# Two decode layers on one core: wq laid out by groups of heads, V 4 and V 5 in unbroken rows, the first K ahead of wq, and K 8 of layer 2 in two transfers

## The chip, the cores and the metric

The kernel runs on one core of a Trainium2 chip. Its time is the device time of one execution in microseconds (us); the time before is the median of three runs. The core has a matrix engine (TensorE, called PE in the profile, with its weight loads as PEld), a vector engine (DVE), a scalar engine (ACT), GpSimd (POOL) and a queue that issues transfers (SP, SPq in the profile). Sixteen DMA engines move data between the device's main memory and the core's on-chip memory, which is addressed by 128 partitions. All transfers of this kernel are issued by SP, in the order in which its instructions stand.

## The reference: what is computed

One token (a row of 640 numbers) goes through two equal layers. Every layer is an attention over a window of a key/value cache and a small feed-forward mixer. Both layers use the same caches and the same weights, and everything is bf16.

```python
W = 4096                                     # the last 4,096 of 32,768 positions
def _A_ref(x, k_cache, v_cache, wq, wo):     # x [1,1,640], caches [1,32,32768,192]
    q = (x @ wq) -> 32 heads of 192          # wq [640, 6144]
    scores = q . k_cache[head, last W] * 192**-0.5
    p = softmax(scores)
    o = p . v_cache[head, last W]
    return o.reshape(1, 1, 6144) @ wo        # wo [6144, 640]
def _B_ref(x, w1, w2, w3, w4):               # w3 [640, 1536], w4 [1536, 640]
    ...
    return x1 + gelu(layernorm(x1) @ w3) @ w4

x = x + _A_ref(_layernorm(x), ...)           # layer 1
x = x + _B_ref(_layernorm(x), ...)
x = x + _A_ref(_layernorm(x), ...)           # layer 2, the same caches and weights
x = x + _B_ref(_layernorm(x), ...)
```

One head's window of keys is 4,096 x 192 bf16, 1.5 MB, and so is its window of values. Thirty-two heads have 96 MB, two layers 192 MB.

## The kernel before

The code counts layers from 0; this text says layer 1 and layer 2 (`layer == 0` and `layer == 1`). "K 8" is the window of keys of head 8, "V 4" the window of values of head 4.

**Tiles.** A window is kept as a tile of 128 partitions x 6,144 numbers (12,288 B in a partition; partition p has 32 positions that follow each other). Twelve such tiles, the cells, are handed round: a loader takes a free cell (`take`), and the work that reads it last gives it back (`give`). wq has a tile of its own, `wq_sb` (L143): 128 partitions x 5 blocks of rows (kc, 0 to 4) x 6,144 columns, 61,440 B in a partition. The 6,144 columns are 8 groups (c, 0 to 7) of 768, four heads each. In the order before, a partition holds kc first and the columns second, so that one group's columns are five pieces of 1,536 B, 12,288 B apart.

**The work of a group.** The query of four heads is projected from wq's columns of that group (`qproj_steps`), the keys of each head are transposed in place on DVE (L534), multiplied with the query on PE (L620), the softmax of the four heads is taken, and the values are summed with its weights (`pv`, L761). wo's rows of the group finish it. Layer 1 takes the groups from 7 down to 0, layer 2 from 0 up to 7.

**What layer 2 finds in place.** Layer 1 ends with heads 0 to 7, and layer 2 begins with them. Their eight K stay in cells as they are. Of the V, V 2 and V 3 stay whole, V 1 and V 4 in part: of V 4 only the first 1,536 of its 6,144 columns have to be loaded again. The space for that, and for V 5, is wq's own: once layer 2 has projected group 0 and then group 1, their columns of wq are not used any more. `fill_hole` (L188) puts three transfers there, at places that `hole` (L182) finds: V 4's 1,536 columns into the first two pieces of group 0's space, V 5's first 2,304 columns into the other three, V 5's other 3,840 columns into the five pieces of group 1's space. Called V 4, V 5a and V 5b below.

**How transfers are issued.** Three forms stand in the code. The plain one, `nc.sync.dma_start`, reads and writes one run for each partition. `load_wide` (L48) joins four partitions' rows into one run of the source, 49,152 B, and spreads it over four partitions. `load_runs` (L59) reads one run for each partition and writes it as several pieces of 1,536 B. Whole cells and wq's blocks kc 1 to 4 go by `load_wide`, wq's block kc 0 and K 8 of layer 2 (`load_k`, L171, with `NKEEP` = 8) by the plain form, and the three parts of V 4 and V 5 by `load_runs`.

**The order.** `stream` (L385) is a written-out list of loads; `need` walks it and issues each item when the program comes to it. It begins with wq's block 0, x, wq's blocks 1 to 4, then K 28, K 29 and so on. An issue waits until its cell is free (for PE and DVE, by semaphores) and until the transfer eight places before it has landed, as eight semaphores are used in turn. At the change of layers the order is: w3 and w4 of layer 1's mixer, V 0 in two halves, two parts of V 1 (3,072 and 768 B in a partition), V 4, V 5a, K 8, K 9, K 10, V 5b, V 6. V 4 and V 5a wait for the projection of layer 2's group 0 (L565), K 8, K 9 and K 10 for the scores (L620) of heads 0, 1 and 2, whose cells they take, and V 5b for the projection of group 1.

Of the kernel before, what the change touches and what calls it, by code (L numbers as in the profile page):

```python
# [9 lines left out]
BF16 = mybir.dt.bfloat16  # L10
# [8 lines left out]
P = 128  # L19
# [29 lines left out]
def load_wide(nc, dst, src):  # L49


    wide = src.rearrange("(g w) n -> g (w n)", w=WIDE)
    assert [list(d) for d in wide.ap] == [[WIDE * src.shape[1], P // WIDE], [1, WIDE * src.shape[1]]]
    sym = [mybir.BassSymbolicTensorAccessPattern(ap=a.ap, dtype=a.dtype, bass_ap=a) for a in (wide, dst)]
    return nc.sync.add_instruction(mybir.InstDMACopy(
        name=nc.get_next_instruction_name(), ins=sym[:1], outs=sym[1:], queue="qSPDynamicHW", mode="Copy"))


def load_runs(nc, dst, src):  # L59

    sym = [mybir.BassSymbolicTensorAccessPattern(ap=a.ap, dtype=a.dtype, bass_ap=a) for a in (src.unsqueeze(1), dst)]
    return nc.sync.add_instruction(mybir.InstDMACopy(
        name=nc.get_next_instruction_name(), ins=sym[:1], outs=sym[1:], queue="qSPDynamicHW", mode="Copy"))
# [3 lines left out]
def kernel(  # L67
# [14 lines left out]
    nc = tc.nc  # L82
    shrink_ring(nc)
    _, _, D = A_x.shape
    _, H, Sk, Dh = A_k_cache.shape
    W = min(4096, max(256, Sk // 4))
    F = B_w3.shape[1]
    HD = H * Dh
# [3 lines left out]
    ND, NF = D // P, F // P  # L92
# [3 lines left out]
    NG = H // QH  # L96
    QC = QH * Dh
    QT = QC // P
# [3 lines left out]
    FREE = NT * HALF  # L102
    scale = float(Dh) ** -0.5
    eps = 1e-5
    s0 = Sk - W
# [3 lines left out]
    NKEEP, NCELL = 8, 12  # L109
# [9 lines left out]
    GROUPS = [[list(range(h, h + QH)) for h in range(0, H, QH)] for _ in range(2)]  # L119
# [9 lines left out]
    fixed = ctx.enter_context(tc.tile_pool(name="fixed", bufs=1))  # L129
# [10 lines left out]
    nc.scalar.add_instruction(mybir.InstLoadActFuncSet(  # L140
        name=nc.get_next_instruction_name(), act_func_set_id=ACT_TABLE_SET, ins=[], outs=[]))

    wq_sb = fixed.tile([P, ND, HD], BF16, name="wq_sb")  # L143
    wx_sb = fixed.tile([P, (ND - W3C) * F + (NF - W4C) * D], BF16, name="wx_sb")

    kx = fixed.tile([P, NKX * Dh], BF16, name="kx")
# [7 lines left out]
    def take(key):  # L154
        i = free.popleft()
        cell_of[key] = i
        return (low if i == NCELL - 1 else cells).tile([P, FREE], BF16, tag=f"cell{i}", name=f"cell{i}")
# [4 lines left out]
    def load(dst, src, wide=True):  # L162
        (partial(load_wide, nc) if wide else nc.sync.dma_start)(dst, src)
# [6 lines left out]

    def load_k(layer, h):  # L171
        t = take(("k", layer, h))
        load(t[:], A_k_cache[0, h, s0:Sk, :].rearrange("(p j) d -> p (j d)", p=P), (layer, h) != (1, NKEEP))
        return t

    SLOT = 2 * Dh
    HOLE = ND * QC
# [1 line left out]
    VYA = HOLE - (FREE - VN)  # L179
    assert QC == 2 * SLOT and (FREE - VN) % QC == 0 and VYA < FREE <= VYA + HOLE  # L180

    def hole(i):  # L182

        c, i = divmod(i, HOLE)
        k, i = divmod(i, QC)
        return wq_sb[:, k, c * QC + i:c * QC + i + SLOT]

    def fill_hole(i, src):  # L188
        c, i = divmod(i, HOLE)
        k, n = i // QC, src.shape[1] // QC  # L190
        assert i % QC == 0 and n * QC == src.shape[1] and k + n <= ND
        load_runs(nc, wq_sb[:, k:k + n, c * QC:(c + 1) * QC], src)

    def load_hole(layer, h):

        src = A_v_cache[0, h % H, s0:Sk, :].rearrange("(p j) d -> p (j d)", p=P)
        if h == VX:
            fill_hole(0, src[:, 0:FREE - VN])
            return hole
        if h == VY + H:  # L200
            fill_hole(FREE - VN, src[:, 0:VYA])
        else:
            fill_hole(HOLE, src[:, VYA:])
        return lambda i: hole(i + FREE - VN)
# [46 lines left out]
        return V[:, i:i + n]  # L251

    def load_wq(layer, kc):
        load(wq_sb[:, kc, :], A_wq[kc * P:(kc + 1) * P, :], kc > 0)
        return wq_sb

    def load_wo(layer, c):
# [32 lines left out]
    def load_w4(layer):  # L290
# [38 lines left out]
        return block  # L329

    LOADERS = {"x": load_x, "k": load_k, "v": load_v, "wq": load_wq, "wo": load_wo, "fill": fill_wo, "w3": load_w3, "w4": load_w4}

    def layer_stream(layer):
# [48 lines left out]
            assert seq[0:4] == [("v", 1, 0), ("v", 1, 1), ("v", 1, VX), ("v", 1, VY + H)]  # L382
        return seq

    stream = [("wq", 0, 0), ("x",)] + [("wq", 0, kc) for kc in range(1, ND)] + layer_stream(0) + layer_stream(1)  # L385
    pos = [0]

    def need(*key):
        while key not in loaded:
            k = stream[pos[0]]  # L390
            pos[0] += 1
            loaded[k] = LOADERS[k[0]](*k[1:])
        return loaded[key]
# [146 lines left out]
    def qproj_steps(c, xc, part=None, row=None):  # L540


        held = {}
        n = QT if part is None else QT // 2
        t0 = c * QT + (part or 0) * n

        def project():
            need("wq", 0, ND - 1)
            if row is not None:
                N = QC // 2  # L550
                qr_ps = psm.tile([33, N], F32, tag="psm")
                for kc in range(ND):
                    for i in range(2):
                        nc.tensor.matmul(  # L554
                            qr_ps[32 * i:32 * i + 1, :], lhsT=xc[:, kc:kc + 1],
                            rhs=wq_sb[:, kc, t0 * P + i * N:t0 * P + (i + 1) * N],
                            start=(kc == 0), stop=(kc == ND - 1))
                for i in range(2):
                    nc.scalar.copy(row[32 * i:32 * i + 1, :], qr_ps[32 * i:32 * i + 1, :])  # L559
                return  # L560
            qT_ps = psm.tile([P, n], F32, tag="psm")
            for tl in range(n):
                t = t0 + tl
                for kc in range(ND):
                    nc.tensor.matmul(  # L565
                        qT_ps[:, tl:tl + 1], lhsT=wq_sb[:, kc, t * P:(t + 1) * P], rhs=xc[:, kc:kc + 1],
                        start=(kc == 0), stop=(kc == ND - 1))
            held["q"] = qT_ps

        def spread():  # L570
            if row is not None:
                qT_ps = psm.tile([P, n], F32, tag="psm")
                for tl in range(n):
                    i, j = divmod(tl, n // 2)
                    nc.tensor.matmul(qT_ps[:, tl:tl + 1], lhsT=row[:, j * P:(j + 1) * P],  # L575
                                     rhs=Eq[0:33, i, 0:1], start=True, stop=True)
                held["q"] = qT_ps
            Xq = o_bytes[:, 2 * (256 + 2 * QH):][:, 0:4 * n].rearrange("p (t b) -> p t b", b=4)
            nc.vector.tensor_tensor(  # L579
                out=Xq[:], in0=held["q"][:, :].unsqueeze(2).broadcast_to([P, n, 4]),  # L580
                in1=maskq[:, :].unsqueeze(1).broadcast_to([P, n, 4]), op=ALU.mult)
            held["x"] = Xq

        def repeat():
            Qrep_ps = psm.tile([P, 4 * n], F32, tag="psm")
            nc.tensor.matmul(Qrep_ps[:], lhsT=Lb[:], rhs=held["x"][:].rearrange("p t b -> p (t b)"),
                             start=True, stop=True)
            held["r"] = Qrep_ps

        def block():  # L590
            nh = n * P // Dh
            h0 = 4 * (t0 - c * QT) // NCOL
            src = held["r"][:, :].rearrange("p (h f) -> p f h", h=nh)
            pairs = [Qblk[:, c % 2, i:i + QPAIR].rearrange("p (f u b) -> p f u b", u=5, b=NM) for i in (0, QPAIR)]
            outer, inner = slice(0, 5, 4), slice(1, 5, 3)
            if nh == QH:
                parts = (pairs[0][:, :, outer], src[:, :, 0:4:3]), (pairs[1][:, :, inner], src[:, :, 1:3])
            else:
                units = (0, 0), (1, 1), (1, 4), (0, 4)
                parts = [(pairs[k][:, :, u:u + 1], src[:, :, i:i + 1]) for i, (k, u) in enumerate(units[h0:h0 + nh])]  # L600
            for to, q in parts:
                shape = [P, NCOL, q.shape[2], NM]
                nc.vector.tensor_tensor(
                    out=to, in0=q.unsqueeze(3).broadcast_to(shape),
                    in1=blkm[:, :].unsqueeze(1).unsqueeze(1).broadcast_to(shape), op=ALU.mult)

        return project, spread, repeat, block

    def scores(h, K, ST, hq):
# [679 lines left out]
```

## Time and profile before

| | us |
|---|---|
| time, median of 3 runs | 510.49 (510.01 to 510.89) |
| the profiled execution: device time | 509.65 |
| its span, from the first to the last instruction | 507.9 |
| DVE busy in the span | 304.1 (60%) |
| PE busy in the span | 277.7 (55%) |

The page of the profile gives the busy time of each engine, then the span in 40 slices of 12.7 us with the share of time in which the 16 DMA engines were busy and the rate at which they moved data, the DMA queues, the chain of work that ended last, and groups of instructions. Other views answer questions of the trace: the windows view gives busy time, DMA share and rate in stretches that one names, the timeline one engine's instructions in order of time, the DMA view the issues with their size and the median time from issue to landing. In the windows view a packet's bytes are put to the moment at which it begins, so that stretches of 1 us with large packets swing, and stretches of several us are read. The trace also holds a record of each DMA packet, with its beginning, its duration and its size.

### The profile page before, as it was taken

The numbers are of one execution on the slowest core, as the hardware profiler recorded it, in microseconds if no ns is written. First come the engines' busy times: TensorE is split into PE (matmuls) and PEld (weight loads), VectorE is DVE, ScalarE is ACT, GpSimd is POOL, SyncE is SP. The second block draws the span as 40 slices with busy tenths as digits, with TensorE's granted clock in tenths as the row PEclk, the third lists the DMA queues.
The fourth block names the chain that finished last, engine by engine and source line by source line (L and its number), as shares of the span: only waits on it lengthen the run. The fifth ranks groups of instructions, "written<-read, shape, count | busy, mean of one in ns | idle before, by whom it ended". The sixth has DMA issues, their size and how long they took to land. (4 is left out here: it accounts for less than half of the span.)

```text
span 507.9 us, 7504 instructions
## 1 busy us (share of the span) xinstructions
PE 277.7 (55%) x3141; PEld 132.9 (26%) x3141; DVE 304.1 (60%) x508; ACT 54.5 (11%) x179; POOL 3.7 (1%) x16
## 2 busy tenths in 40 slices
PE   1134747536274473853756666647463753637675
PEld 0011313213031131311423543223121221212145
DVE  2076686567674675746735365867766665756532
ACT  1000101011010110100011101011110101001111
POOL 2000000000000000000000000000000000000000
PEclk9995695758767687585775595978877785766655
DMA  9999999999999999999999999999999999999996
GB/s 372 434 434 434 431 442 431 400 430 433 443 432 441 428 421 437 426 411 446 431 389 421 359 396 446 431 430 431 430 425 437 434 423 434 421 448 431 418 401 250
DMA packets 12725, 213.41 MB, mean 420 GB/s; under 512 B 2804, under 2 KB 3444, under 8 KB 8436
## 3 DMA queue, kind: packets, MB, share of 16 engines
q1 hardware_dynamic: 12692, 212.94, 98.6%
q8 instruction: 25, 0.41, 0.3%
q14 instruction: 8, 0.07, 0.0%
HBM read 212.93 MB, written 0.00 MB: 419 GB/s over the span
## 5 line engine op out<-in xcount | busy, mean ns | idle before, releaser
L534 DVE STREAM_TRANSPOSE cell<-cell 128x1536 uint32<-128x1536 uint32 (+1 forms) x83 | 193.3, 2331 | 33.6 <-DMA cell<-in_A_k_cache_dram 32.9
L620 PE MATMUL ST_ps<-cell,Qblk 128*16 128x512 bf16 (+1 forms) x864 | 134.1, 473 | 83.9 <-DVE cell L534 68.3
L761 PE MATMUL O_ps<-cell,PT 128*2 128x384 bf16 x916 | 90.0, 424 | 5.9 <-DMA cell<-in_A_v_cache_dram 2.8
L620 PEld LDWEIGHTS <-Qblk 128*16 128x16 bf16 x864 | 43.9, 104 | 145.3 <-issue 121.3
L770 DVE STREAM_TRANSPOSE o_sb<-O_ps 128x384 f32<-128x384 f32 x60 | 33.8, 563 | 45.5 <-PE O_ps L761 45.5
L783 ACT ACTIVATE words<-oT_ps,words 32x6 bf16<-32x6 f32 x63 | 16.2, 257 | 245.6 <-PE oT_ps L782 149.8
L761 PEld LDWEIGHTS <-PT 128*2 128x2 bf16 x1024 | 34.2, 92 | 30.2 <-issue 19.5
L579 DVE TENSOR_TENSOR o_sb<-qT_ps,words 128x24 bf16<-128x24 f32 (+1 forms) x17 | 3.0, 179 | 47.0 <-PE qT_ps L575 45.7
L657 PE MATMUL pmT_ps<-ident,words 64*1 64x64 f32 (+1 forms) x16 | 4.1, 257 | 42.9 <-DVE words L652 42.8
L554 PE MATMUL qr_ps<-wq_sb,words 128*1 128x384 bf16 x120 | 20.4, 484 | 11.5 <-DMA wq_sb<-in_A_wq_dram 10.5
L782 PE MATMUL oT_ps<-o_sb,Lq 128*32 128x6 f32 x126 | 14.3, 186 | 22.4 <-DVE o_sb L781 22.4
L782 PEld LDWEIGHTS oT_ps<-o_sb,Lq 128*32 128x32 f32 x126 | 12.1, 126 | 40.7 <-issue 26.9
L684 DVE STREAM_TRANSPOSE o_sb<-o_sb 64x512 bf16<-64x512 bf16 (+1 forms) x14 | 9.4, 669 | 19.9 <-ACT o_sb L678 18.6
L809 PE MATMUL yr_ps<-cell,words 128*1 128x320 bf16 x120 | 16.1, 431 | 0.0
L673 PE MATMUL nb_ps<-words,o_sb 1*64 1x1 f32 (+1 forms) x14 | 2.6, 185 | 24.5 <-DVE o_sb L665 24.4
L657 PEld LDWEIGHTS pmT_ps<-ident,words 64*1 64x1 f32 (+1 forms) x16 | 1.2, 77 | 45.4 <-issue 44.3
L652 DVE TENSOR_REDUCE words<-ST_ps 64x1 f32<-64x512 f32 (+1 forms) x16 | 10.3, 643 | 3.6 <-PE ST_ps L620 3.5
L559 ACT CAST wx_sb<-qr_ps 1x384 bf16<-1x384 f32 x16 | 7.5, 468 | 43.9 <-PE qr_ps L554 28.3
L781 DVE TENSOR_TENSOR o_sb<-o_sb 128x6 f32<-128x6 f32 x63 | 10.7, 170 | 2.0
L554 PEld LDWEIGHTS <-words 128*1 128x1 bf16 x120 | 6.6, 109 | 19.6 <-issue 17.1
L678 ACT ACTIVATE o_sb<-ST_ps,o_sb,words 64x512 bf16<-64x512 f32 (+1 forms) x14 | 10.4, 743 | 0.5
L675 ACT COPY o_sb<-nb_ps 64x1 f32<-64x1 f32 (+1 forms) x14 | 2.1, 153 | 74.1 <-PE nb_ps L673 74.1
(184 smaller groups left out, 192.0 us busy)
## 6 DMA issues: line engine op xcount, KB each, us to landing
cell<-in_A_k_cache_dram SPq DMA_DIRECT2D x56, 1536.0 KB, 27.7
cell<-in_A_v_cache_dram SPq DMA_DIRECT2D x53, 1536.0 KB, 27.8
cell<-in_A_wo_dram SPq DMA_DIRECT2D x13, 960.0 KB, 27.7
wq_sb<-in_A_wq_dram SPq DMA_DIRECT2D x5, 1536.0 KB, 12.1
cell<-in_A_v_cache_dram SPq DMA_DIRECT2D x8, 768.0 KB, 15.8
cell<-in_B_w_dram SPq DMA_DIRECT2D x4, 768.0 KB, 9.1
cell<-in_A_wo_dram SPq DMA_DIRECT2D x3, 480.0 KB, 16.9
cell<-in_B_w_dram SPq DMA_DIRECT2D x2, 640.0 KB, 10.1
```

The lines of the kernel that those rows point to most:

```text
L534: nc.vector.transpose(Ku, Ku)
L554: nc.tensor.matmul(qr_ps[32 * i:32 * i + 1, :], lhsT=xc[:, kc:kc + 1], rhs=wq_sb[:, kc, t0 * P + i * N:t0 * P + (i + 1) * N], start=(kc == ...
L620: nc.tensor.matmul(ST_ps[r:r + QW, :].rearrange("p (g j i) -> p g j i", g=ng, j=NJ4), lhsT=Q[n], rhs=T[:, ng * i:ng * (i + 1), :, f, :, t] ...
L652: nc.vector.tensor_reduce(out=pm[S, :], in_=ST_ps, op=ALU.max, axis=AX.X)
L678: nc.scalar.activation(out=Pr, in_=ST_ps, func=ACTF.Exp, bias=nb_sb[:, 0:1], scale=sc[S, 0:1], accum_out=lpart[:, 0:1])
L684: nc.vector.transpose(held["PrT"], held["Pr"])
L761: nc.tensor.matmul(O_ps[r:r + 2, :], lhsT=PT[:, hq, 2 * i:2 * i + 2], rhs=v_pair(V, h, 2 * i * Dh, 2 * Dh), start=(i < 4), stop=(i >= NB - 4))
L770: nc.vector.transpose(o_sb[:], O_ps.rearrange("p (e a c) -> p e c a", e=2, c=NA))
L781: nc.vector.tensor_add(o2, o2, o_sb[:, 1, :, 1])
L782: nc.tensor.matmul(oT_ps[r, :], lhsT=Lq[:], rhs=o2, start=True, stop=True)
L783: nc.scalar.activation(oT[r, :], oT_ps[r, :], ACTF.Copy, scale=rl[r, 0:1])
L809: nc.tensor.matmul(yr_ps[32 * i:32 * i + 1, :], lhsT=oT[:, k:k + 1], rhs=wo_t[:, k * D + i * N:k * D + (i + 1) * N], start=(k == 0), stop= ...
```

## The change

- `wq_sb` becomes 128 partitions x 8 groups x 5 blocks x 768 columns: a partition now holds one group after the other, 7,680 B each. PE reads the same 1,536 B pieces at other places, and the space of a projected group is one unbroken run.
- V 4, V 5a and V 5b then are one run in each partition, of 3,072, 4,608 and 7,680 B, and go by the plain form.
- wq's blocks kc 1 to 4 still go by `load_wide`, and each 49,152 B run of the source is now written as 32 pieces of 1,536 B where it was 4 of 12,288 B. Block kc 0 becomes two transfers: the columns of group 7, 1,536 B in a partition, by the plain form, and the other seven groups by `load_runs`, 10,752 B read and seven pieces written.
- The first K of the stream, K 28, goes ahead of everything, by the plain form where it was wide. x stays second, and then come wq's blocks.
- K 8 of layer 2 becomes two plain transfers, of 3,072 and 9,216 B in a partition.

The instructions of PE, DVE, ACT and POOL and their order are the same. SP issues two transfers more than before.

```diff
@@ load_wide
     wide = src.rearrange("(g w) n -> g (w n)", w=WIDE)
+    wide = wide.unsqueeze(1) if len(dst.shape) == 3 else wide
@@
-    wq_sb = fixed.tile([P, ND, HD], BF16, name="wq_sb")
+    wq_sb = fixed.tile([P, NG, ND, QC], BF16, name="wq_sb")
@@ load_k
         t = take(("k", layer, h))
-        load(t[:], A_k_cache[0, h, s0:Sk, :].rearrange("(p j) d -> p (j d)", p=P), (layer, h) != (1, NKEEP))
+        src = A_k_cache[0, h, s0:Sk, :].rearrange("(p j) d -> p (j d)", p=P)
+        if (layer, h) == (1, NKEEP):
+            for i, e in ((0, FREE // 4), (FREE // 4, FREE)):
+                nc.sync.dma_start(t[:, i:e], src[:, i:e])
+        else:
+            load(t[:], src, (layer, h) != (0, GROUPS[0][0][0]))
         return t
@@
-    def hole(i):
+    def hole(i, n=SLOT):
         c, i = divmod(i, HOLE)
-        k, i = divmod(i, QC)
-        return wq_sb[:, k, c * QC + i:c * QC + i + SLOT]
+        return wq_sb[:, c].rearrange("p k n -> p (k n)")[:, i:i + n]
     def fill_hole(i, src):
-        c, i = divmod(i, HOLE)
-        k, n = i // QC, src.shape[1] // QC
-        assert i % QC == 0 and n * QC == src.shape[1] and k + n <= ND
-        load_runs(nc, wq_sb[:, k:k + n, c * QC:(c + 1) * QC], src)
+        nc.sync.dma_start(hole(i, src.shape[1]), src)
@@
     def load_wq(layer, kc):
-        load(wq_sb[:, kc, :], A_wq[kc * P:(kc + 1) * P, :], kc > 0)
+        rows = A_wq[kc * P:(kc + 1) * P, :]
+        if kc > 0:
+            load_wide(nc, wq_sb[:, :, kc, :], rows)
+        else:
+            nc.sync.dma_start(wq_sb[:, NG - 1, kc, :], rows[:, HD - QC:])
+            load_runs(nc, wq_sb[:, 0:NG - 1, kc, :], rows[:, 0:HD - QC])
         return wq_sb
@@
-    stream = [("wq", 0, 0), ("x",)] + [("wq", 0, kc) for kc in range(1, ND)] + layer_stream(0) + layer_stream(1)
+    seq = layer_stream(0) + layer_stream(1)
+    stream = [seq.pop(0), ("x",)] + [("wq", 0, kc) for kc in range(ND)] + seq
@@ qproj_steps
-                            rhs=wq_sb[:, kc, t0 * P + i * N:t0 * P + (i + 1) * N],
+                            rhs=wq_sb[:, c, kc, i * N:(i + 1) * N],
...
-                t = t0 + tl
+                t = t0 - c * QT + tl
                 for kc in range(ND):
                     nc.tensor.matmul(
-                        qT_ps[:, tl:tl + 1], lhsT=wq_sb[:, kc, t * P:(t + 1) * P], rhs=xc[:, kc:kc + 1],
+                        qT_ps[:, tl:tl + 1], lhsT=wq_sb[:, c, kc, t * P:(t + 1) * P], rhs=xc[:, kc:kc + 1],
                         start=(kc == 0), stop=(kc == ND - 1))
```

## The prediction

> **What bounds the kernel now.** I read the page first: how busy each engine is, the slices, the DMA queues.
>
> ```profile
> span 507.9 us, 7504 instructions
> PE 277.7 (55%) x3141; PEld 132.9 (26%) x3141; DVE 304.1 (60%) x508; ACT 54.5 (11%) x179; POOL 3.7 (1%) x16
> ...
> DMA  9999999999999999999999999999999999999996
> GB/s 372 434 434 434 431 442 431 400 430 433 443 432 441 428 421 437 426 411 446 431 389 421 359 396 446 431 430 431 430 425 437 434 423 434 421 448 431 418 401 250
> ...
> q1 hardware_dynamic: 12692, 212.94, 98.6%
> ```
>
> No engine is over 60% busy, and the DMA engines are busy in every slice: the end is set by 213 MB, their rate and the stretches in which it sinks. The lowest slices are the last (the tail of the last mixer) and the 23rd, 279 to 292 us, the change of layers. The windows view, cut finer there and with two long stretches beside it, gives (after the busy times: PE clock, DMA share, GB/s):
>
> ```profile
> 20.00:260.00 240.00, 128.50 (x1196) 56.82 (x1195) 155.60 (x201) 25.15 (x77) 0.00 (x0) 0.73 1.00 431
> 354.00:480.00 126.00, 68.81 (x661) 28.43 (x655) 82.84 (x110) 12.56 (x40) 0.00 (x0) 0.73 1.00 431
> ```
> ```profile
> 288.00:290.00 2.00, 1.84 (x33) 1.05 (x37) 0.49 (x5) 0.00 (x0) 0.00 (x0) 0.50 0.83 249
> 290.00:292.00 2.00, 2.00 (x42) 1.32 (x34) 0.05 (x1) 0.29 (x2) 0.00 (x0) 0.61 1.02 357
> 292.00:294.00 2.00, 2.00 (x70) 1.45 (x62) 0.69 (x4) 0.18 (x1) 0.00 (x0) 1.00 0.93 239
> 294.00:296.00 2.00, 1.26 (x30) 0.78 (x26) 0.65 (x3) 0.00 (x0) 0.00 (x0) 1.00 0.93 387
> ```
>
> Against 431, 288 to 290 is short of 364 KB (0.84 us), and 290 to 296 of 618 KB (1.43 us). SP's timeline shows what it issued then (start, duration):
>
> ```profile
> 281.40 4.57 SPq L216 DMA_DIRECT2D cell<-in_A_v_cache_dram  x4
> 287.80 1.24 SPq L62 DMA_DIRECT2D wq_sb<-in_A_v_cache_dram  x2
> 289.66 0.34 SPq L163 DMA_DIRECT2D cell<-in_A_k_cache_dram  x1
> 291.18 1.80 SPq L55 DMA_DIRECT2D cell<-in_A_k_cache_dram  x2
> 293.32 0.56 SPq L62 DMA_DIRECT2D wq_sb<-in_A_v_cache_dram  x1
> ```
>
> V 4 goes at 287.80, as soon as PE has projected group 0 (30 matmuls of L565 from 286.91 to 287.85), and takes 0.59 us to issue; V 5a follows at 288.48, 0.55; K 8 at 289.66, when PE is through with head 0. By the packet records most DMA engines have no packet between 288.6 and 289.2. K 8's first packets of 12,288 B begin between 292.2 and 292.8 and take 1.04 to 1.81 us where 0.46 is usual: its data flow from about 292.9, 3.2 us after the issue. At the kernel's start the plain wq block, of the same shape, is issued at 0.74 and flows from about 2.5, 1.8 us later; V 0's second half, issued at 283.84, after 1.9. So K 8 is some 1.3 us late, behind V 4 and V 5a with their 640 pieces. From 300 to 474, by issues against packet records, 16 us and more of transfers are always issued ahead: time that DMA loses here is lost at the end, and time that it wins is kept.
>
> **The change part by part.** Terms are per DMA engine, as all sixteen work side by side.
>
> *V 4 and V 5 plain.* Plain issues (V 0's, L216) take 0.33 us, V 4's 0.59. V 4 stands at the head of an empty queue, so its data come 0.26 earlier: -0.26. Then the 1.43 us. V 5a's packets average 210 ns, 178 without a stall (8 packets, 0.25 us), K 8's 555 against 460 (8, 0.76), and between V 5a's last and K 8's first packet engines stand empty for 0.34 on average: 1.35; the rest is the fixed part of small packets and stays. No row shows K 8 behind two plain transfers here. Bounds: all 1.35 goes, or none. The nearest row is V 1's first part, plain, issued at 285.04 behind plain halves with 2.4 us of transfers ahead (K 8 has 2.3): four engines of sixteen stalled for 0.3 to 0.45 us, 0.13 on average. I take that: -1.22. PE's order and waits are the same, so K 8 can't be issued before 289.66; what is late next is PE's chain from the mixer's last product to the projection, which leaves the remaining 0.6 us of 288 to 290 as it is.
>
> *K 8 in two.* Eight packets more. The line through packets of 1,280 B (55 ns) and 2,560 B (102 ns) leaves 8 ns a packet: +0.06. The second issue costs SP 0.4 us; K 9 stands behind it, at 291.18, and waits for PE. The transposition needs both parts.
>
> *wq in pieces.* V 5b, five pieces a packet, averages 293.6 ns where a plain packet of 7,680 B takes 291: 0.65 ns a further piece. A wide wq packet gets 28 more: 4 transfers x 2 packets x 28 x 0.65 = 0.15; block 0 has 8 packets with 6 more, 0.03, and 8 packets more, 0.06. V 5b itself: -0.02. Bounds for a piece: nothing, or 8 ns, as for a packet of its own (272 pieces, 2.2 us). I take 0.65, from the row of the same form.
>
> The Trainium skill, DMA: Bandwidth & Descriptors, section on the semaphore's increment of 16, says that one descriptor moves one contiguous run, and its table of measured loads has about 10.5 ns a packet; an estimate from these, 3,712 runs more over 16 engines, is 2.4 us, against 0.22 by V 5b's row.
>
> *K 28 first, and plain.* 8 packets of 460 ns for 2 of 1,820: +0.04. x stays second behind 1.5 MB, so DVE's L476 stays at 6.80. wq's last block lands at about 25.3 instead of 21.6 and Qblk is written at 28.1 instead of 24.4. The transposition of K 28 (3.38 us) starts then instead of at 25.30, K 29's ends at 34.9 instead of 32.3; the third started at 34.81 in any case, behind 2.45 us of waiting for ACT. The lag is gone there, and cost nothing while 21 us and more of transfers are issued ahead. SP issues two transfers more before K 29, which waits for K 28 to land (about 7) as it did for wq's block before. The cells go round as before, one transfer ahead in the ring of eight.
>
> Sum: -0.26 - 1.22 + 0.06 + 0.22 + 0.04 = -1.16, some 508.5 on the profiled execution's own 509.65 (span 507.9 and 1.75 around it). That execution lies 0.84 under the median; on the median 510.49 it is 509.3. I call 0.2% (1.0 us) what a measurement here tells from no change.
>
> **The rivals.**
>
> *Pieces are described slower than they are moved* (slower). If K 8 was late because 640 pieces had to be described ahead of it, wq's pieces must be too, 1,024 in a transfer. The 1.3 us over the 384 pieces beyond one a row make 3.4 ns each: 3.5 us a transfer, against 3.64 to move it, and K 28 gives a lead of some 2.7. That just holds; it turns at 3.5 ns. Counted from V 4's issue to 1.0 us before K 8's first packet (the delay at the kernel's start), 288.0 to 291.2, all time to 640 pieces, it is 5 ns: 5.1 us a transfer, 1.5 late four times, 1.3 in block 0, less the lead: 4.6 later, less the gain of 1.2 at the change of layers: 513.9. Halfway between the two prices, 511.6. For it: the two prices stand so near to each other. Against: issue takes 0.55 to 0.59 us for two, three and five pieces a row alike.
>
> *K 8's stall is its own* (no change): engines that run dry need a microsecond to restart, whatever was ahead. Then -0.26 and +0.32 remain: 510.55. Against: V 1 and V 0 restarted in half the time.
>
> The Trainium skill, Perfetto Trace Analysis, HWDGE's DMA instruction, says that descriptors are generated within the issue's profiled span; by that V 5a was described by 289.03, and this rival would hold. The start of the kernel, 0.6 us from the issue's end to the first packet, can't decide it.
>
> *Each piece costs like a packet* (slower): 2.2 us for 0.18, 511.3. Against: V 5b's row. For it: that row was behind others, at a rate of 424 GB/s, and has five pieces where wq has 32. The Trainium skill's figure above belongs here.
>
> **How the numbers follow.** The forecast, 509.3, has 0.54, of which 0.42 lies over 0.2% faster; descriptions too slow 0.24; K 8's own stall 0.13; dear pieces 0.07; 0.02 for other gains. So faster 0.44, same 0.24, slower 0.32. The forecast's own range is 508.6 to 510.1 (all of the stall gone and free pieces, to half of it). The range reaches past the middle of the slower rival: 508.6 to 512.6 leaves out some 0.06 below and 0.14 above.
>
> **What would show it.** Right: windows 290 to 296 at 400 GB/s or more, K 8's first data within 2 us of its issue, plain issues of 0.33 us at V 4 and V 5a, 3 to 25 us at 430 as before, wq's last block landing at about 25.3. Wrong: slices 1 and 2 below 430 with wq's transfers 4 to 5 us apart (pieces described too slowly), wide wq packets well over 1.84 us (dear pieces), or K 8's first packets again over 1 us with the same hole at 292 (its own stall).

## The result, and the profile after

The changed kernel takes 511.33 us (median of 21 runs, 510.47 to 512.05), the kernel before 510.22 in the same comparison (21 runs, 509.38 to 512.13). The ratio is 1.0016, with a 95% interval from 1.0009 to 1.0023: 0.5 to 1.2 us slower. The forecast was 509.3, 1.2 us faster. A later comparison of the same two kernels gave 1.0014 (1.0002 to 1.0027).

The page of the changed kernel: busy engines, slices, DMA queue.

```profile
span 508.9 us, 7508 instructions
PE 282.7 (56%) x3141; PEld 135.9 (27%) x3141; DVE 303.5 (60%) x508; ACT 54.6 (11%) x179; POOL 3.7 (1%) x16
...
DMA  9999999999999999999999999999999999999995
GB/s 371 425 433 433 434 390 435 442 433 430 444 427 433 431 427 410 433 430 449 430 387 420 357 406 441 447 431 415 433 434 444 422 430 433 412 435 430 424 409 226
...
q1 hardware_dynamic: 13076, 212.94, 98.6%
```

The DMA engines are still the bound, and the 23rd slice, the change of layers, is still low: 357 GB/s for 359. The second slice, 13 to 25 us, has fallen from 434 to 425. The windows view of the changed kernel, in the stretches that the prediction read (the sixth row is the three before it together), and from 6 to 25 us, where wq moves behind K 28 (the kernel before has 456 there, but its large packets begin elsewhere at the edges; the lag below is the cleaner measure):

```profile
20.00:260.00 240.00, 129.43 (x1190) 57.90 (x1189) 154.96 (x200) 25.19 (x77) 0.00 (x0) 0.72 1.00 429
288.00:290.00 2.00, 1.73 (x49) 1.27 (x46) 0.79 (x5) 0.11 (x2) 0.00 (x0) 0.50 1.01 333
290.00:292.00 2.00, 2.00 (x34) 0.94 (x26) 0.27 (x2) 0.00 (x0) 0.00 (x0) 0.50 0.87 292
292.00:294.00 2.00, 2.00 (x35) 1.28 (x36) 0.15 (x1) 0.46 (x2) 0.00 (x0) 0.50 1.03 263
294.00:296.00 2.00, 2.00 (x51) 1.32 (x48) 0.54 (x3) 0.00 (x0) 0.00 (x0) 0.50 1.00 387
290.00:296.00 6.00, 6.00 (x113) 3.54 (x105) 0.96 (x6) 0.46 (x2) 0.00 (x0) 0.50 0.96 314
6.00:25.00 19.00, 2.75 (x11) 1.01 (x12) 1.81 (x8) 0.30 (x2) 0.00 (x0) 1.00 1.02 422
```

290 to 296 us was to reach 400 GB/s and has 314 (328 before). At 292 to 294 the engines are busy all the time and move 263: packets that take long, not engines without packets. By the packet records K 8's first packets, of 3,072 B now, begin between 292.4 and 293.2, and ten of them take 0.4 to 1.55 us where 0.12 is usual. SP's timeline shows that the issues did become short, V 4 and V 5a 0.81 us together for 1.24 before, and that K 8 goes 1.86 us after V 4, as before:

```profile
288.59 0.81 SPq L194 DMA_DIRECT2D wq_sb<-in_A_v_cache_dram  x2
290.45 0.80 SPq L177 DMA_DIRECT2D cell<-in_A_k_cache_dram  x2
291.96 2.38 SPq L56 DMA_DIRECT2D cell<-in_A_k_cache_dram  x2
```

At the start, SP's timeline of the changed kernel, and below it that of the kernel before:

```profile
2.73 12.18 SPq L56 DMA_DIRECT2D wq_sb<-in_A_wq_dram  x4
14.95 5.71 SPq L56 DMA_DIRECT2D cell<-in_A_k_cache_dram  x4
```
```profile
1.61 2.51 SPq L55 DMA_DIRECT2D wq_sb<-in_A_wq_dram  x4
4.16 7.07 SPq L55 DMA_DIRECT2D cell<-in_A_k_cache_dram  x5
```

Four issues of wq take 12.2 us instead of 2.5; the last three, 3.7 to 4.0 us each, are about as long as a transfer takes to move, so it looks as if SP waits for room. The engines have packets throughout. But by the packet records each wide wq packet takes 1.886 us in place of 1.820, all of them alike, and PE can use wq's last block at 26.0 us, where the forecast has 25.3.

To follow such small sums I use one more reading of the packet records: the *lag*, the time by which a kernel reaches the same number of moved bytes later than the profile of the kernel before. For the changed kernel it is 0.05 us at 6.5, grows evenly to 0.66 at 24, is 0.73 from 150 to 261, and 0.33 at 300. At the end of the chain of waits, the landing of w3 that PE waits for (kernel before, then the changed one):

```profile
490.77 10.24 DMA cell<-in_B_w_dram
501.01 0.05 issue
501.06 0.49 PE V_ps L1181 x12
```
```profile
491.69 10.31 DMA cell<-in_B_w_dram
502.00 0.05 issue
502.05 0.50 PE V_ps L1190 x12
```

The landing is 0.99 us later, though the packets of w3 end only 0.30 later on average (497.72 for 497.42): the last engine is later than the mean one.

### The profile page after: what moved, and what is told of

Read it like the earlier page. It is cut to its first block, busy times and chain, and to the rows that moved or that the text cites. A ratio compares the mean times of both kernels' runs of the same rounds, so it can differ in the third digit from the quotient of the medians.

```text
span 508.9 us, 7508 instructions
## 1 busy us (share of the span) xinstructions
PE 282.7 (56%) x3141; PEld 135.9 (27%) x3141; DVE 303.5 (60%) x508; ACT 54.6 (11%) x179; POOL 3.7 (1%) x16
## 5 line engine op out<-in xcount | busy, mean ns | idle before, releaser
L629 PE MATMUL ST_ps<-cell,Qblk 128*16 128x512 bf16 (+1 forms) x864 | 138.3, 494 | 73.6 <-DVE cell L543 57.9
L629 PEld LDWEIGHTS <-Qblk 128*16 128x16 bf16 x864 | 45.2, 108 | 137.8 <-issue 115.4
L770 PEld LDWEIGHTS <-PT 128*2 128x2 bf16 x1024 | 35.5, 92 | 31.3 <-issue 20.3
```

The lines of the kernel that those rows point to most:

```text
L629: nc.tensor.matmul(ST_ps[r:r + QW, :].rearrange("p (g j i) -> p g j i", g=ng, j=NJ4), lhsT=Q[n], rhs=T[:, ng * i:ng * (i + 1), :, f, :, t] ...
L770: nc.tensor.matmul(O_ps[r:r + 2, :], lhsT=PT[:, hq, 2 * i:2 * i + 2], rhs=v_pair(V, h, 2 * i * Dh, 2 * Dh), start=(i < 4), stop=(i >= NB - 4))
```

## The experiments

Four questions: which part costs, what a piece costs, why K 8's first packets are long, and whether the mean engine or the last one counts.

### Which part: layout alone, order and split alone, K 8 in one

Layout alone (`e1`): the changed kernel with the stream's order and K 8 as before.

```diff
-    seq = layer_stream(0) + layer_stream(1)
-    stream = [seq.pop(0), ("x",)] + [("wq", 0, kc) for kc in range(ND)] + seq
+    stream = [("wq", 0, 0), ("x",)] + [("wq", 0, kc) for kc in range(1, ND)] + layer_stream(0) + layer_stream(1)
...
```

> wq by groups and V 4, V 5 in unbroken rows alone; the stream's order (wq ahead, K 28 wide, fifth) and K 8 in one transfer are as before. Theory A (the loss is made by wq's pieces: the wide wq packets took 1.886 us for 1.820, 8 of them on each engine, 0.53 us, and the last engine to finish sets the end): a wide wq packet takes 1.88 to 1.89 us again, and the kernel is 0.4 to 1.0 us slower than before, ratio 1.0008 to 1.002. Theory B (the loss is made by the order or by K 8's split, the pieces' cost is made good at the change of layers): 0 to 0.6 us faster than before, ratio 0.9988 to 1.000.

Measured: 513.37 for 510.68, ratio 1.0054 (1.0039 to 1.0070). Worse than either theory had it. Wide wq packets take 1.886 us, as theory A says, but there is a loss ahead of them: the lag is 1.04 us at 6.5, and 1.63 at 26. Windows view of this kernel (the kernel before has 424 GB/s in this stretch, the changed one 412):

```profile
3.00:5.00 2.00, 0.00 (x0) 0.00 (x0) 1.31 (x10) 0.00 (x0) 0.56 (x2) 1.00 0.76 258
```

Another 1.7 came at 261 to 275 us (lag 1.70 to 3.41), in the slowest of the six executions; a step of this kind is no mark of the layout, as a second profile of the kernel before has one too (the last experiment). What can be put down to the order is the start: with K 28 ahead of wq the lag is 0.05 to 0.15 at 6.5 us and 0.73 to 0.89 at 250, and without it 1.04 and 1.67, some 0.8 to 0.9 us more. K 8 in one transfer, the other difference, costs nothing that can be told (`e3`).

Order and split alone (`e2`): the kernel before with K 28 first and K 8 in two.

```diff
-    stream = [("wq", 0, 0), ("x",)] + [("wq", 0, kc) for kc in range(1, ND)] + layer_stream(0) + layer_stream(1)
+    seq = layer_stream(0) + layer_stream(1)
+    stream = [seq.pop(0), ("x",)] + [("wq", 0, kc) for kc in range(ND)] + seq
...
-        load(t[:], A_k_cache[0, h, s0:Sk, :].rearrange("(p j) d -> p (j d)", p=P), (layer, h) != (1, NKEEP))
+            for i, e in ((0, FREE // 4), (FREE // 4, FREE)):
+                nc.sync.dma_start(t[:, i:e], src[:, i:e])
```

> K 28 first and plain, and K 8 in two transfers, in the kernel before with wq in its old order. Theory A (the pieces): within 0.3 us of before, ratio 0.9994 to 1.0006, with wide wq packets of 1.82 us. Theory B (order or split): 0.6 to 1.4 us slower, ratio 1.0012 to 1.0027.

Measured: 510.90 for 510.68, 1.0008 (0.9997 to 1.0018); the lag is 0.03 at 250 us. In the old layout these two parts cost nothing that can be told. The times alone would not tell this kernel from the changed one; the lag does.

K 8 in one (`e3`):

```diff
-            for i, e in ((0, FREE // 4), (FREE // 4, FREE)):
-                nc.sync.dma_start(t[:, i:e], src[:, i:e])
+        load(t[:], src, (layer, h) not in ((0, GROUPS[0][0][0]), (1, NKEEP)))
```

> The changed kernel with K 8 of layer 2 in one plain transfer. If K 8's stall is its own, whatever stands ahead and however it is cut: its first packets, now of 12,288 B, take 1.0 us and more on several engines as in both kernels, and the time is within 0.3 us of the changed kernel's, ratio to before 1.001 to 1.0022. If the split makes the stall (the packets of 3,072 B took up to 1.55 us): packets near 0.46 us, some 0.5 us or more faster than the changed kernel, ratio 1.0006 or less.

Measured: 511.25 for 510.68, 1.0010 (0.9999 to 1.0021), and K 8's packets up to 1.89 us for 0.46, a mean of 571 ns. The cut of K 8 doesn't make its stall.

### What a piece costs

Rows of 12,288 B in eight pieces (`e4`), and all blocks as block kc 0 is (`e8`):

```diff
-            load_wide(nc, wq_sb[:, :, kc, :], rows)
+            load_runs(nc, wq_sb[:, :, kc, :], rows)
```

> The changed kernel with wq's blocks kc 1 to 4 read one row a partition (128 packets of 12,288 B, each written in eight pieces) where it is four rows (32 packets of 49,152 B in 32 pieces). The number of pieces is the same, 1,024 a transfer. If a piece costs 2.4 ns in any packet (66 ns for 28 further pieces): a packet takes 0.477 us, 0.70 us more on each engine than plain wide packets, 0.17 more than the changed kernel, ratio 1.0012 to 1.0027. If a piece costs what block kc 0 shows (10,752 B in seven pieces at about 0.404 to 0.408 us, under 0.8 ns a piece) and the cost is one of the wide packet: 0.463 to 0.466 us a packet, 0.2 to 0.35 us faster than the changed kernel, ratio 1.0006 to 1.0014.

Measured: 511.44 for 510.68, 1.0017 (1.0009 to 1.0026); packets of 475 ns where plain ones take 460: 2.1 ns a further piece.

> The changed kernel with wq's blocks kc 1 to 4 loaded as block kc 0 is: group 7's columns in a plain transfer (1,536 B a partition) and the other seven groups as 10,752 B read and seven pieces written. If seven pieces a packet are free, as block kc 0 shows (404 ns, and 403 by the line through plain packets of 7,680 and 12,288 B): 0.404 us a packet in all blocks, 65 ns for the small ones, 3.75 us a block where the wide one took 3.77: the same time within 0.3 us, 511.3 plus or minus 0.8 in a single run. If a piece costs 2.1 to 2.4 ns in every block but the first: 0.415 to 0.42 us a packet.

Measured: 511.27 in one run; 416 ns for 10,752 B in seven pieces, where the line through plain packets gives 403: 2.2 ns a piece. Block kc 0 itself, 404 for most of its packets, looks like an exception, but only its first packets are free of the price: in the order in which they begin, the first 80 of the changed kernel's 128 take 404 ns for the most part, the next 16 mostly 407, and of the last 32 most take 416, again 2.2 ns a further piece. V 5b in the kernel before, the row from which the prediction had its price, has the same two values: the first 32 packets take 291 ns like a plain one, and of the last 32 most take 299, 2 ns for each of the four further pieces. The kernel before with K 28 first (`e2`) and the changed one with V 5 in pieces (`e11`) show the same in V 5b. What makes the first packets free, no run shows.

Half pieces (`e7`): everything doubled, 2,048 pieces of 768 B in a transfer.

```diff
-    wq_sb = fixed.tile([P, NG, ND, QC], BF16, name="wq_sb")
+    wq_sb = fixed.tile([P, 2 * NG, ND, QC // 2], BF16, name="wq_sb")
...
```

> The changed kernel with wq in 16 half groups of 384 columns: every piece is 768 B where it was 1,536, a wide packet of 49,152 B is written in 64 pieces (32 before), a packet of block kc 0 in 14 (7); group 7's part of block kc 0 goes plain in packets of 768 B. A group's space stays one run, and the V are unchanged. Theory A (2.1 to 2.4 ns a further piece): wide wq packets of 1.95 to 1.97 us for 1.886, 0.5 to 0.7 us more on each engine, ratio to before 1.0022 to 1.0034. Theory B (pieces are described slower than they are moved: SP's issues of wq lasted 3.67 to 3.97 us with 1,024 pieces, and the engines just kept up): 2,048 pieces take 7 us and more a transfer, the engines starve from about 9 us on, 10 us or more lost by 30 us, ratio 1.015 or more.

Measured: 511.98 for 510.60, 1.0033 (1.0017 to 1.0049); wide packets of 1.964 us, 144 ns over plain for 60 further pieces, 2.4 ns each, as 66 ns for 28 are in the changed kernel. The price goes by the number of pieces. Block kc 0 shows it as well: with 14 pieces its first packets take 404 ns again and most of the later ones 435. SP's timeline of this kernel:

```profile
2.85 16.30 SPq L56 DMA_DIRECT2D wq_sb<-in_A_wq_dram  x4
```

An issue now takes 4.0 to 4.2 us with twice the pieces, again about what the transfer takes to move (3.93), and the lag grows evenly, to 1.53 at 24 us. The engines have packets throughout, so 2,048 pieces are described in the 3.93 us or less, 1.9 ns each at most, and description isn't what holds these transfers up. Theory B falls, and with it the first rival as long as something stands ahead of wq.

The Trainium skill, DMA: Bandwidth & Descriptors, in the section on the semaphore's increment of 16, has one descriptor for each contiguous run, and the note at its table of measured loads, which GpSimd issued, has about 10.5 ns a packet. Here a piece of the write side costs 2.1 to 2.4 ns: where the read is one run, its figure for packets, put on pieces, is four to five times too much.

### Why K 8's first packets are long

V 4 and V 5 in pieces again, into the same space (`e11`), beside the changed kernel once more:

```diff
-        nc.sync.dma_start(hole(i, src.shape[1]), src)
+        load_runs(nc, hole(i, src.shape[1]).rearrange("p (k n) -> p k n", n=QC), src)
```

> The changed kernel with V 4, V 5a and V 5b issued in pieces of 1,536 B again, to the same unbroken space. My prediction's step (without pieces K 8's stall of 1.2 us and 0.26 us of V 4's issue go): undone, 1.2 to 1.5 us slower than the changed kernel, ratio to before 1.004 to 1.005. Theory A (only the issue is shorter, the stall is not the pieces'): V 4's issue takes 0.55 to 0.6 us again, and the time is 0 to 0.5 us slower than the changed kernel, ratio 1.001 to 1.0027.

> The changed kernel once more, as the other side of the previous run and for a second profile: ratio to before 1.0008 to 1.0024, wide wq packets of 1.886 us, 0.7 to 0.9 us of lag in the bytes moved at 250 us, and a first packet of K 8 of over 1 us.

Measured: 511.21 for 510.60, 1.0017 (1.0007 to 1.0026), and the changed kernel 511.55, 1.0014 (1.0002 to 1.0027). SP's timeline with the pieces back, 1.22 us for the two issues:

```profile
288.73 1.22 SPq L63 DMA_DIRECT2D wq_sb<-in_A_v_cache_dram  x2
290.59 0.98 SPq L177 DMA_DIRECT2D cell<-in_A_k_cache_dram  x2
```

K 8's packets of 3,072 B average 208 ns with pieces ahead of them and 210 without (208 in the first profile), the longest 1.65 and 1.46 us. K 8's second part, packets of 9,216 B that usually take 347 ns, averages 382 with pieces ahead and 361 and 355 without, some 0.2 us on each engine at most. The pieces are not the cause of the stall, and bringing them back costs no time that can be told, where the prediction's step asks for 1.2 to 1.5 us. The kernel before had shown such a stall without any pieces: V 0's packets of 6,144 B, all plain, take up to 0.90 us at 285 to 286 us where 0.234 is usual.

V 5a longer (`e5`), so that engines have work until K 8 can come:

```diff
...
+        a, b = (x.rearrange("p (k two n) -> p two k n", two=2, n=P) for x in (hole(i, n), src))
+        for j in range(2):
+            nc.sync.dma_start(a[:, j], b[:, j])
```

> The changed kernel, with V 5a read in 18 packets of 256 B a partition (two transfers, which interleave) where it is one of 4,608 B. By the row of the 256 B packets (18 ns) that is 144 packets, 2.6 us on each engine for 1.42, so the engines still move V 5a when K 8's first packets can begin, 2.0 us after its issue. Theory A (K 8's first packets are long because the engines ran dry before them): the first packets of K 8 (3,072 B) take under 0.6 us, the added 1.2 us stand in place of the empty time and the stall, and the time is within 0.5 us of the changed kernel's, ratio to before 1.0005 to 1.0026. Theory B (the stall belongs to K 8, whatever engines do before): packets of 1.4 us and more again, and 1.0 to 1.3 us slower than the changed kernel, ratio 1.0032 to 1.005.

Measured: 511.78 for 510.87, 1.0021 (1.0010 to 1.0033). K 8's packets of 3,072 B average 161 ns, the longest 0.81 us: about half of the stall has gone, and of the added 1.2 us of small packets some 0.3 may be left in the time (1.0021 beside 1.0014 and 1.0016; the intervals overlap). The time is theory A's, the packets lie between the two. Against empty engines as the cause stands the changed kernel itself: there each of the ten packets that take over 0.4 us begins 2 ns after a packet of V 5a has ended. (The records name no engine; so short a distance ten times over is taken as the same one.)

A short transfer at the head of the stream (`e9`), without any pieces:

```diff
-        load(wq_sb[:, kc, :], A_wq[kc * P:(kc + 1) * P, :], kc > 0)
...
+            nc.sync.dma_start(wq_sb[:, kc, HD - QC:], rows[:, HD - QC:])
+            nc.sync.dma_start(wq_sb[:, kc, 0:HD - QC], rows[:, 0:HD - QC])
```

> The kernel before, with wq's block kc 0 in two plain transfers at the head of the stream, first 1,536 B a partition, then 10,752 B; no pieces anywhere in wq. Theory A (a transfer that comes to a short queue pays its own start-up, 2 us and more from its issue to its data, and a short one ahead of it does not cover that; so K 8's stall has nothing to do with pieces): the 10,752 B packets begin at about 2.6 us and the first ones take 0.8 to 1.3 us, and the bytes moved lag 0.7 to 1.1 us behind the kernel before at 6.5 us. Theory B (in the layout alone the pieces of the second transfer made that stall, 1.04 us of lag at 6.5 us): packets near 0.41 us and a lag under 0.3 us.

Measured, in one run of 511.61 us: the 10,752 B packets begin at 2.44 us, and ten of them take 0.7 to 1.06, but the lag at 6.5 us is only 0.15. Theory A's price was wrong: the kernel before pays for such a start too, its first packets of 12,288 B take up to 1.29 us for 0.46, so little is added. So the 1.04 us of `e1` do belong to pieces that stand at the very head of the stream; whether it is their description or their writing wasn't separated.

K 8's source, its form and its place (the diffs of the first and the third; in the second the two transfers become one wide one):

```diff
+        cache = A_v_cache if (layer, h) == (1, NKEEP) else A_k_cache
```

> The changed kernel with K 8 of layer 2 read from V's cache, the window of head 8 (so the keys of head 8 are not the reference's in layer 2; shapes, sizes and order are unchanged). Theory S (the source: the first K after a stretch of V alone is slow to read): K 8's first packets of 3,072 B stay under 0.5 us, their mean near 130 ns instead of 208 to 213. Theory T (a transfer that finds little ahead of it has a start-up of its own, from wherever it reads): some 8 to 12 of the first packets at 0.4 to 1.7 us again, mean near 208.

> The changed kernel with K 8 of layer 2 as one wide transfer, 32 packets of 49,152 B. Theory F (the stall comes with the many small packets at a transfer's head, in any form of 128 rows): wide packets of 1.82 to 1.9 us in K 8. Theory T (start-up of the transfer): K 8's first wide packets take up to 1.2 to 1.5 us longer, 2.5 to 3.4 us, on several engines.

```diff
-            assert seq[0:4] == [("v", 1, 0), ("v", 1, 1), ("v", 1, VX), ("v", 1, VY + H)]
+            seq[3], seq[4] = seq[4], seq[3]
```

> The changed kernel with K 8 ahead of V 5a: V 4, K 8 in two, V 5a, K 9. K 8 can't be issued before head 0's scores (290.4), so engines stand empty longer and the time rises by up to 1.4 us. Theory T (start-up): K 8's first packets begin 1.0 to 1.2 us after its issue on engines that are empty, and are stalled by 0.3 to 1.3 us as V 4's are; V 5a, with K 8 ahead of it, has packets of 0.18 us without a stall. Theory K (the stall is tied to K 8's own place in the program or its cell): V 5a free of it and K 8's packets 1.4 us and more, ending at about 294.2 as before.

Measured, one run each: 511.31, 510.94 and 510.87, and the kernel before 512.19, also in one run; only packets and lag are read from these. From the other cache the stall is the same (232 ns on average, up to 1.79 us): not the source. In the wide form eleven of K 8's 32 packets take 2.68 to 3.39 us for 1.82: not the form. With K 8 ahead of V 5a its first packets begin 1.0 us after the issue and take 0.4 to 0.97 us, two packets of its second part 1.7 and 2.2 for 0.35, V 5a's average 183 ns, almost without a stall, and the lag, 1.34 us at 292 with engines standing empty, is back at 0.50 at 300: the stall isn't tied to K 8's place in the program, and what is lost in empty engines at 292 is won back by 300. So the likeliest reading is theory T: a transfer that finds little ahead of it has a start of its own, which a deep queue hides and 2 us of work ahead do not. What the start consists of, no run shows.

### The last engine, and the kernel before once more

Three packets more on one engine (`e6`):

```diff
...
+    i = stream.index(("k", 1, 20))
+    stream[i:i] = [("dup", 0), ("dup", 1), ("dup", 2)]
```

> The changed kernel with three more transfers of one packet each (49,152 B of V into space of wq that is not used any more), ahead of K 20 of layer 2, at about 370 us. Bytes by the mean: 147 KB more at 431 GB/s, 0.34 us. Theory A (an engine that falls behind stays behind, and the last one sets the end): if the three packets go to one engine, it is 5.5 us later, less what it was ahead of the slowest (up to 3 us), so that the kernel is 2.5 to 5.5 us slower than the changed kernel, ratio to before 1.0065 to 1.0125. Theory B (the engines' mean sets the end): 0.3 us slower than the changed kernel, ratio 1.0015 to 1.003.

Measured: 516.64 for 510.87, 1.0115 (1.0100 to 1.0131), with 0.07% more bytes. The chain of waits has w3's landing at 507.39, 5.39 us later than in the changed kernel, and three packets of 1.82 are 5.46:

```profile
497.07 10.32 DMA cell<-in_B_w_dram
507.39 0.05 issue
507.44 0.49 PE V_ps L1201 x12
```

From 502.8 us on the last packets of w3 end 0.12 us apart, as long as one of them takes: a single engine is still at work. So the three went to one engine, what it fell behind was not made good in the 120 us that followed, and the last engine set the end. That agrees with the section of the Trainium skill's page that was named above (DMA: Bandwidth & Descriptors, on the semaphore's increment of 16), by which the engines of a transfer finish independently and the semaphore counts them all.

The kernel before, once more:

> The kernel before once more, for a second profile of it: how much the last engine's end differs from one execution to the next. If the stalls fall on other engines each time: the last w3 packet of the tail ends up to 1 us away from 500.71, the mean of their ends within 0.2 us of 497.42.

Measured: 511.43 us, 1.8 more than its first profile. Up to 261 us the two profiles agree to 0.1 us of lag (0.01 at 261); at 268 the second is 0.94 behind, and stays so (0.97 at 300). The last w3 packet ends at 502.11 (500.71). The means differ too, by 1.0 (498.40 for 497.42), which the expectation didn't have. In this execution K 8 has almost no stall (474 ns on average for 460), V 5a has it (232 ns for 178), and the engines stood emptier. Windows view of this second profile, where the first has 249 and 357 in the first two rows:

```profile
288.00:290.00 2.00, 1.51 (x43) 1.28 (x46) 1.21 (x7) 0.30 (x2) 0.00 (x0) 0.50 0.80 276
290.00:292.00 2.00, 2.00 (x41) 1.08 (x34) 0.27 (x2) 0.00 (x0) 0.00 (x0) 0.50 0.64 189
292.00:294.00 2.00, 2.00 (x49) 1.30 (x38) 0.15 (x1) 0.47 (x2) 0.00 (x0) 0.75 0.76 224
```

The step at 261 to 268 us can be followed back to PE's clock. The windows view of the first profile, and below it of the second:

```profile
241.00:247.00 6.00, 5.17 (x60) 3.12 (x62) 3.38 (x9) 0.52 (x2) 0.00 (x0) 0.73 0.93 401
263.00:265.00 2.00, 0.70 (x20) 0.56 (x17) 0.25 (x3) 0.26 (x1) 0.00 (x0) 0.50 0.65 240
```
```profile
241.00:247.00 6.00, 5.24 (x51) 3.55 (x55) 3.19 (x8) 0.27 (x1) 0.00 (x0) 0.50 0.93 401
263.00:265.00 2.00, 1.28 (x36) 1.07 (x33) 0.84 (x4) 0.24 (x1) 0.00 (x0) 0.50 0.47 94
```

With the granted clock at 0.50 instead of 0.73, PE's twelve matmuls of L831 at 241.4 us take 2.26 us for 1.34, and PE stays behind. SP waits 3.0 us for PE (L761) where it waited 1.7, issues the next four transfers (L236) at 263.19 instead of 261.90, and the engines have less to move until then (94 GB/s for 240). The same wait is 2.9 to 3.9 us, the clock 0.50 and the step there in the second profile of the changed kernel, in `e1` and in `e9`; in the other thirteen profiles the clock of this stretch is 0.66 to 0.78, and none has the step. How often the timed runs have it isn't known. So two profiles of one kernel differ by 1 us from there on; before 261 us a profile tells 0.1 us, behind it only the timed runs tell the order. The lag about 250 us, good to some 0.05, is the cleanest sum of the first half:

| kernel | lag about 250 us | ratio to before |
|---|---|---|
| before, second profile | 0.02 | - |
| order and split alone (`e2`) | 0.03 | 1.0008 |
| short head, no pieces (`e9`) | 0.15 | - |
| changed, two profiles | 0.73, 0.89 | 1.0016, 1.0014 |
| K 8 in one (`e3`), V in pieces (`e11`) | 0.89, 0.91 | 1.0010, 1.0017 |
| rows of eight pieces (`e4`), of seven (`e8`) | 0.92, 0.88 | 1.0017, - |
| half pieces (`e7`) | 1.62 | 1.0033 |
| layout alone, wq ahead (`e1`) | 1.67 | 1.0054 |

Every kernel with wq in pieces has 0.7 us or more, and those without have 0.15 or less.

## Why the prediction was wrong

- **V 4's issue, -0.26.** The issue took 0.33 us as forecast. Its gain is too small to be told in the times (`e11`).
- **V 5a and K 8's stall, -1.22: the step that failed.** It took V 1's first part, stalled by 0.13, as the nearest row for K 8 behind two plain transfers. K 8 kept its stall (packets 88 ns over the usual 121 on average, eight on each engine: 0.7 us), with or without pieces ahead. V 0's packets at 285 us, stalled by up to 0.67, were the row that showed it. The second rival, the stall is K 8's own, was right about the stall, except that empty engines alone are not its cause; its time, 510.55, has the same small price for pieces. Between 268 and 300 us the changed kernel gained 0.25 us of lag in one profile and 0.66 in the other, where 1.48 was forecast, and with the pieces back (`e11`) it gained 0.26 as well, so that even this gain isn't shown to come from the plain form.
- **K 8 in two, +0.06, and K 28 first, +0.04.** Both hold within what can be told (`e2`, `e3`). But the prediction counted K 28's lead only in a rival, and it was worth 0.8 to 0.9 us of lag: as much as the price of all the pieces. The ratio without it, 1.0054, is larger still, and the runs don't show how much of that is the step at 261 us.
- **wq in pieces, +0.22: a term mis-sized.** 0.65 ns a piece, from V 5b's 293.6 ns, was the average of first packets that take 291 like plain ones and last ones that take 299, 2 ns a further piece. wq's wide packets are all of the second kind: 2.4 ns. The four wide blocks cost 8 x 66 ns = 0.53 us, block kc 0 and the start the rest of 0.73 to 0.89.
- **Descriptions too slow.** This rival, the largest, fell: even 2,048 pieces a transfer were described in time (`e7`). Something like it may hold where wq stands at the head (`e1`). **Pieces as dear as packets** fell as well: 2.4 ns, not 8.
- **"All sixteen work side by side".** The sum went by the mean engine. A stall that falls on five engines and not on eleven counts in full at the end if the last engine is among them, as the three packets of `e6` do, so a mean taken over all sixteen can understate stalls, and overstate what a shorter mean wins.
- **The base.** The sum was put on a profile 0.84 us under the median. The second profile of the same kernel differs by 1 us from 268 on, by the clock that PE was granted some 20 us before.

With what the runs gave, the sum is +0.73 to +0.89 for the first half, and -0.25 to -0.66 at the change of layers: +0.1 to +0.6. Measured is +0.5 to +1.2. The remainder, a few tenths, may be the last engine's share or the step at 261 us, if the timed runs meet it more often in one kernel; the runs don't separate it. No kernel tried here was faster than the kernel before.

## What to carry to other kernels

A layout that makes a rare small transfer unbroken is paid where the large transfer is written: count the pieces on the write side, price them with packets of the same form, late ones and early ones apart, and double them once to see that the price is linear. Before a stall is put down to what stands ahead of it, look for the same stall where that cause is absent, and profile the kernel before a second time to learn which differences are its own. What one DMA engine loses, the end can lose in full, and what PE loses to its clock, the transfers that wait for PE can lose too.

## What was not expected of the hardware

- A write piece of 768 or 1,536 B inside a packet that reads one run costs 2.1 to 2.4 ns, in packets of 10,752, 12,288 and 49,152 B alike, but the first packets of two transfers went free of it: some 80 of block kc 0's 128 (404 ns for 403, the last ones 416) and some 80 of V 5b's 128 (291 ns as plain ones, the last ones 299).
- SP's issue of a transfer lasted 3.7 to 4.2 us, with 1,024 and with 2,048 pieces, where 0.5 to 0.6 is usual for wide ones, about as long as a transfer took to move (3.77 and 3.93). Nothing was lost by it here, as the engines had packets throughout.
- With about 2 us of transfers ahead a transfer's first packets take up to 1.7 us longer than usual (1.79 us for 0.12 in `e12`), in three forms and from both caches, even where a packet of the transfer ahead has ended just before.
- One engine that is given three packets of 1.82 us more ends the kernel 5.4 us later, with 120 us of work still ahead of it.
- A granted clock of 0.50 instead of 0.73 over 6 us of PE's work made four transfers go 1.3 us later some 20 us on, and cost a DMA-bound kernel 0.9 us in its profile.
